# Pooled values times w_in: three float32r passes over split operands, or plain float32 products in the halves of a PSUM bank

## The chip, the cores and the metric

The kernel runs on one core of a Trainium2 chip. The metric is device time in microseconds (us); less is better. PE is TensorE, DVE is VectorE, ACT is ScalarE, POOL is GpSimd, and SP is the engine that issues the loads and stores here.

## The reference

```
a   = softmax(phi, axis=2)                       # over 576 positions, for each of 32 memory slots
k_m = einsum('bhsm,bhsd->bhmd', a, k)            # pooled keys,   32 x 64 per head
v_m = einsum('bhsm,bhsd->bhmd', a, v)            # pooled values, 32 x 64 per head
attn = softmax(q @ k_m.T / sqrt(64))             # 576 x 32 per head
x   = (attn @ v_m), heads side by side           # 2304 x 512
h   = x @ w_in; g = maximum(0.01 * h, h); y = g @ w_out          # d_ff 2048
out = ((y @ w_a) * (y @ w_b)) @ w_out2                           # d_ff 1536
```

There are 4 batches, 8 heads, and 2304 tokens (576 for each batch). Weights reach the kernel as 64-bit words, which it turns into float32 itself.

## The kernel before

**The tiling.** x is never formed. For each batch b and each chunk c of 512 columns of w_in (c = 0 to 3), the kernel multiplies the pooled values of the 8 heads by their rows of w_in. The result vw has 8 heads x 32 slots = 256 rows and 512 columns. Then h = attn @ vw (`h_unit`, L794) and y += g @ w_out (`y_unit`, L826) run over blocks of 288 tokens, two to a batch. The second MLP (`ab_unit`, `left_unit`, `o_unit`, `o_part`) follows.

**The split.** A product of full float32 accuracy is made of float32r operands: each is split into a high part (a copy that rounds to float32r) and a low part (the rest, by a subtraction), and PE makes three passes, high x high, high x low and low x high. So `weight` (L462) first joins the two words of each value into a float32 tile `cv` (loads by SP, two activations on ACT, then clamp, shift, join and add on DVE, some of them on POOL). Then it makes the split tile `win` of it (`hi` L501, `lo` L504). The pooled values are split into `vm_hi` and `vm_lo` (`ev_hi` L621, `ev_lo` L625), and vw itself into `vwh` and `vwl` when it leaves PSUM. The scores q @ k_m.T (`sc_part`, L661) and the pooling (`k_m`, L581) are plain float32 products without a split. `s_sc` writes two of them, of 64 rows each, into the two halves of one PSUM bank.

**The products in question.** A pair of heads has 64 rows of pooled values (32 slots for each head, the other head's half being zero). There are two ways before the change. For batches 0 and 1 in chunk 0, `vw_pair` (L723) fills a bank of 128 rows with two pairs: POOL copies the split values into tiles padded to 128 columns (`vp_hi`, `vp_lo`; `pad_hi`, `pad_lo`), and six passes of 256 columns add up in one bank. Everywhere else `vw_unit` (L749) takes two batches at a time, 64 rows each, in three passes of 256 (c = 0) or 512 columns. Each unit then leaves PSUM in four instructions of 64 rows, since two batches go to two tiles.

**The order.** All instructions are given to `Program.op` with planned costs, and `Program.order` fixes each engine's order ahead of the run. It goes by due time (`late`, less a slack from the table SLACK), by free tiles, and by the engine that would end sooner where two may do it. So a change of costs or of instructions can move other work. Each engine then runs its own list in order, and waits on semaphores.

**Names.** `ta`, `tz` are transposes of the softmaxed phi, `km` the pooled keys and values of four heads, `kvn` the same divided by the softmax sum, `kvt` its transpose; `kbd` holds the pooled keys for the scores `sc`; `sm`, `mx`, `sr`, `at`, `ahi`, `alo` are the stages of the attention softmax of a block and its split. In names such as `vw_0_1_0_1` the numbers are chunk, batch, column half and head group; in `h_0_2_0` chunk, block of 288 tokens, and quarter of the columns; `ta_1_0` and `sc_1_0_0` begin with the batch.

Of the kernel before, what the change touches and what calls it, by code (L numbers as in the profile page):

```python
# [10 lines left out]
F32 = mybir.dt.float32  # L11
# [13 lines left out]
FC = 512  # L25
# [307 lines left out]
def tile_mem_attention__leaky_mlp__bilinear_mlp(  # L333
# [61 lines left out]
    def two(n):  # L395

        return Port({"DVE": c_dve(n), "POOL": c_pool2(n)})

    def copy_by(n, psum=False):
        return (dict if psum else Port)({"ACT": c_act(n), "DVE": (c_dve(n) if psum else c_dve2(n)) + BIAS})  # L400

    def copy(e, dst, src):
        if e == "ACT":
            nc.scalar.copy(dst, src)  # L404
        else:
            nc.vector.tensor_copy(dst, src)
# [8 lines left out]
            small[key] = st_p.tile([P, cols], F32, name="_".join(map(str, key)))  # L415
        return small[key]

    tile_of(("vm_hi",), "slot", [4, B, 2 * M], F32R)
    tile_of(("vm_lo",), "slot", [4, B, 2 * M], F32R)
    VM = [("vm_hi",), ("vm_lo",)]  # L420


    VP = [("vp_hi",), ("vp_lo",)]
    for k in VP:
        tile_of(k, "slot", [4, 2, 4 * M], F32R)

# [6 lines left out]
    op(
        "POOL", 3.5, zeros,
        w=[("vm", b, g) for b in range(B) for g in range(2)] + [("vp", b, g) for b in range(2) for g in range(2)]
        + [("kbd", i, g) for i in range(2) for g in range(2)],
        tiles=VM + VP,
    )


# [21 lines left out]
    def weight(kind, c, k, after=()):  # L462
# [52 lines left out]
        op(Port({"DVE": 0.62, "POOL": 2.45}), 0, add, r=[("l", key)], w=[a], tiles=[cv], ahead=any_time)  # L515
        if kind in ("wa", "wb"):
            return
        if kind == "wout2" and by_seven(1, c):
            op(
# [5 lines left out]
        op(two(512), 0, lo, r=[a, ("hi", key)], w=[key], tiles=[cv, key], ahead=any_time, slack=SLACK[(kind + "0", k // 2) if first else kind])  # L525


    def kv_part(b, g):
# [84 lines left out]
        def wide(t, i):  # L613

            return [t[i * 64:i * 64 + 64, 2 * g + j, b, 2 * M * j + i * M:2 * M * j + i * M + M] for j in range(2)]

        def ev_k(T, e):
            for i in range(2):
                copy(e, own(kbd[b % 2], i), part(T, 0, i))

        def ev_hi(T, e):  # L621
            for i in range(2):
                copy(e, own(T[VM[0]], i, b), part(T, 1, i))

        def ev_lo(T):  # L625
            for i in range(2):
                nc.vector.tensor_tensor(
                    own(T[VM[1]], i, b), part(T, 1, i), own(T[VM[0]], i, b).bitcast(F32), op=ALU.subtract
                )

        def pad_hi(T):
            for i in range(2):
                for j, d in enumerate(wide(T[VP[0]], i)):
                    nc.gpsimd.tensor_copy(d, own(T[VM[0]], i, b)[:, j].bitcast(F32))

        def pad_lo(T):
            for i in range(2):
                for j, d in enumerate(wide(T[VP[1]], i)):
                    nc.gpsimd.tensor_copy(d, own(T[VM[1]], i, b)[:, j].bitcast(F32))

        op({"DVE": 0.5, "ACT": 0.45}, 0, ev_k, r=[o], w=[("kbd", b % 2, g)], tiles=[o])
        op({"ACT": 0.45, "DVE": 0.5}, 0, ev_hi, r=[o], w=[("vmh", b, g)], tiles=[o, VM[0]])
        op("DVE", 0.5, ev_lo, r=[o, ("vmh", b, g)], w=[("vm", b, g)], tiles=[o, *VM])
        if b < 2:
            op("POOL", 0.5, pad_hi, r=[("vmh", b, g)], w=[("vp", b, g)], tiles=[VM[0], VP[0]])
            op("POOL", 0.5, pad_lo, r=[("vm", b, g)], w=[("vp", b, g)], tiles=[VM[1], VP[1]])

    def q_load(b, g):
        if b > 0:
# [57 lines left out]
        )  # L707


    def vw(c, bs):  # L710

        n = FC if c else FC // 2
        m = len(bs) * 2 * M
        if len(bs) == 1:
            for x in range(2):
                for g in range(2):
                    vw_pair(bs[0], x, g)
            return
        for x in range(FC // n):
            for j in range(4):  # L720
                vw_unit(c, bs, x, j, n, m)

    def vw_pair(b, x, g):  # L723

        n = FC // 2
        o, w = ("vw", 0, b, x, g), ("win", 0, 2 * x + g)
        tile_of(o, "x", [n])
        cols = slice(x * n, (x + 1) * n)
        hk, lk = ("vwh", 0, b), ("vwl", 0, b)
        tile_of(hk, "slot", [2, FC], F32R)  # L730
        tile_of(lk, "slot", [2, FC], F32R)

        def prod(T):
            for j in range(2):
                for k, (v, i) in enumerate(((0, 0), (0, 1), (1, 0))):
                    nc.tensor.matmul(
                        T[o], T[VP[v]][:, 2 * g + j, b, :], T[w][:, i, j * n:(j + 1) * n],
                        start=(j == 0 and k == 0), stop=(j == 1 and k == 2),
                    )

        op("PE", 0.72, prod, r=[w, ("vp", b, g)], w=[o], tiles=[o, w, *VP], ahead=15.0)
        op(copy_by(n, True), 0, lambda T, e: copy(e, T[hk][:, g, cols], T[o]), r=[o], w=[(hk, g, x)], tiles=[o, hk])
        op(
            "DVE", c_dve(n),
            lambda T: nc.vector.tensor_tensor(T[lk][:, g, cols], T[o], T[hk][:, g, cols].bitcast(F32), op=ALU.subtract),
            r=[o, (hk, g, x)], w=[(lk, g, x)], tiles=[o, hk, lk], slack=SLACK["vw", 0, b],
        )

    def vw_unit(c, bs, x, j, n, m):  # L749
        o, w = ("vw", c, bs[0], x, j), ("win", c, j if c else 2 * x + j // 2)  # L750
        tile_of(o, "x", [n])
        cols, wcols = slice(x * n, (x + 1) * n), slice(0, FC) if c else slice(j % 2 * n, (j % 2 + 1) * n)
        to = slice((j % 2) * 64, (j % 2) * 64 + 64)

        def prod(T):
            for k, (v, i) in enumerate(((0, 0), (0, 1), (1, 0))):
                nc.tensor.matmul(  # L757
                    T[o][0:m], T[VM[v]][:, j, bs[0]:bs[0] + len(bs), :].rearrange("p b m -> p (b m)"), T[w][:, i, wcols],
                    start=(k == 0), stop=(k == 2),
                )  # L760

        op("PE", 0.01 + n * 1.27e-3, prod, r=[w] + [("vm", b, j // 2) for b in bs], w=[o], tiles=[o, w, *VM], ahead=15.0)
        for i, b in enumerate(bs):
            hk, lk = ("vwh", c, b), ("vwl", c, b)
            tile_of(hk, "slot", [2, FC], F32R)
            tile_of(lk, "slot", [2, FC], F32R)

            def hi(T, e, i=i, hk=hk):
                copy(e, T[hk][to, j // 2, cols], T[o][i * 64:(i + 1) * 64, :])

            def lo(T, i=i, hk=hk, lk=lk):
                nc.vector.tensor_tensor(  # L772
                    T[lk][to, j // 2, cols], T[o][i * 64:(i + 1) * 64, :], T[hk][to, j // 2, cols].bitcast(F32), op=ALU.subtract
                )

            op(copy_by(n, True), 0, hi, r=[o], w=[(hk, j, x)], tiles=[o, hk])
            op("DVE", c_dve(n), lo, r=[o, (hk, j, x)], w=[(lk, j, x)], tiles=[o, hk, lk], slack=SLACK["vw", min(c, 1), bs[0]])
# [16 lines left out]
    def h_unit(c, n, f, pos):  # L794
# [8 lines left out]
        def prod(T):  # L803
            for k in range(2):
# [490 lines left out]
    for c in range(NC1):  # L1295
        for k in range(4):
            weight("win", c, k)
        for bs in ([0], [1], [2, 3]) if c == 0 else ([0, 1], [2, 3]):
            vw(c, bs)
        for k in range(4):  # L1300
            weight("wout", c, k)
        for n in range(NBLK):
            for f in range(4):
                h_unit(c, n, f, (step, (-6, -5, -3, -1)[f]))
            for e in range(4):
                y_unit(c, n, e, (step + 1, (-4, -2, 0, 1)[e]))
            step += 1
# [80 lines left out]
```

## Time and profile before

| | |
|---|---|
| median of 3 runs | 807.0 us (806.95 to 807.73) |
| profiled execution | 804.98 us, of which the span from first to last instruction is 803.2 us |
| busy in the span | PE 778.4 us (97%), DVE 648.4 (81%), ACT 400.2 (50%), POOL 178.1 (22%) |
| granted TensorE clock | 0.998 of full speed, mean over the span |

"Busy" is the time in which an engine has an instruction in work. Matmuls overlap, so 97% for PE says that it rarely stood still, not that it ran at its peak. The windows and chains of the rows further down say more: they tell in which stretch an engine had gaps, and how long a piece of work took from its start to the start of the next.

### The profile page before, as it was taken

To read this page: it belongs to the slowest core of one execution; us is meant where nothing else is said; L and a number is where in the kernel's file an instruction comes from. 1 tells how busy PE (TensorE), PEld (TensorE's weight loads), DVE (VectorE), ACT (ScalarE), POOL (GpSimd) and SP (SyncE) were. 2 spreads that over 40 slices of the span, in tenths; PEclk is the share of its full clock that TensorE was granted. 3 is DMA by queue.
4 is the path that set the end of the run, shared out by engine and by line. 5 is a ranking of instruction groups with operands and counts; after the bars stand their busy time and mean duration, and the time that the engine had idled before them with its cause. 6 is when DMAs were issued, how large, how long until landed. Compare 5 with 4: busy or idle time off the path is not lost.

```text
span 803.2 us, 13329 instructions
## 1 busy us (share of the span) xinstructions
PE 778.4 (97%) x4898; PEld 695.9 (87%) x4898; DVE 648.4 (81%) x1240; ACT 400.2 (50%) x859; POOL 178.1 (22%) x274
## 2 busy tenths in 40 slices
PE   5789999999999999999999999999999989999998
PEld 4578899999999999999978888888888877888886
DVE  6998898889887988897756998998944665798955
ACT  5756786776657566644335544454411244232120
POOL 4632453033101420530100102341200111034200
PEclk9999999999999999999999999999999999999999
DMA  9995301174226232137887665665597778566402
GB/s 338 326 299 165 119 1 54 42 248 145 72 86 223 94 117 94 64 140 252 292 287 238 220 232 191 215 251 163 198 319 289 281 260 279 194 211 214 152 1 104
DMA packets 55216, 150.01 MB, mean 187 GB/s; under 512 B 6896, under 2 KB 20208, under 8 KB 55152
## 3 DMA queue, kind: packets, MB, share of 16 engines
q1 hardware_dynamic: 55152, 149.18, 53.9%
q8 instruction: 38, 0.62, 0.3%
q14 instruction: 26, 0.21, 0.1%
HBM read 103.55 MB, written 45.61 MB: 186 GB/s over the span
## 4 chain that ended last, share of the span: by engine, by line
PE 85%; DMA 6%; DVE 5%; issue 1%; ACT 1%; SPq 0%; ACTq 0%; DVEq 0%
PE y L836 24%; PE abx L1049 14%; PE o L1135 12%; PE h L806 12%; PE abz L1049 7%; PE os L1251 4%; PE aby L1049 3%; DMA k_yb_T<-yb_T 3%; PE vw L757 2%; PE b L1103 2%; PE a L1103 2%; DMA q<-in_qT_dram 1%; DMA k_wout<-wout 1%; PE sc L674 1%; PE km L586 1%
## 5 line engine op out<-in xcount | busy, mean ns | idle before, releaser
L836 PE MATMUL y<-g,wout 128*128 128x288 f32 x1536 | 219.5, 296 | 0.1
L836 PEld LDWEIGHTS y<-g,wout 128*128 128x128 f32 x1536 | 209.2, 188 | 3.3 <-issue 1.3
L1049 PE MATMUL abx<-yb_T,wo 128*128 128x512 f32 x432 | 110.2, 390 | 0.6 <-ACT t L1060 0.6
L1135 PE MATMUL o<-p,wout 128*128 128x512 f32 x384 | 94.8, 390 | 0.9 <-ACT oacc L404 0.9
L1049 PEld LDWEIGHTS abx<-yb_T,wo 128*128 128x128 f32 x432 | 80.0, 188 | 17.1 <-ACT t L1060 1.2
L1060 ACT COPY t<-abx 128x512 f32<-128x512 f32 x72 | 42.2, 586 | 97.4 <-PE abx L1049 97.4
L783 ACT ACTIVATE g<-h 128x288 fp32r<-128x288 f32 x128 | 52.6, 411 | 70.9 <-PE h L806 64.7
L1135 PEld LDWEIGHTS o<-p,wout 128*128 128x128 f32 x384 | 71.8, 188 | 16.6 <-ACT oacc L404 1.3
L806 PE MATMUL h<-ahi,vwh 128*128 128x288 f32 x256 | 76.9, 300 | 0.8 <-ACT ahi L404 0.8
L806 PE MATMUL h<-alo,vwh 128*128 128x288 f32 x256 | 76.3, 298 | 1.1 <-POOL alo L387 1.0
L806 PE MATMUL h<-ahi,vwl 128*128 128x288 f32 x256 | 76.0, 297 | 0.0
L848 DVE TENSOR_TENSOR acc<-y,acc 128x288 f32<-128x288 f32 x96 | 43.2, 454 | 19.6 <-PE y L836 18.6
L822 DVE TENSOR_TENSOR g<-t,g 128x288 fp32r<-128x288 f32 x100 | 48.5, 487 | 5.1 <-ACT t L783 4.7
L783 ACT ACTIVATE t<-h 128x288 f32<-128x288 f32 x128 | 52.1, 407 | 0.1
L806 PEld LDWEIGHTS h<-ahi,vwh 128*128 128x128 f32 x256 | 48.7, 190 | 3.1 <-issue 1.5
L806 PEld LDWEIGHTS h<-alo,vwh 128*128 128x128 f32 x256 | 48.7, 190 | 1.8 <-POOL alo L387 1.7
L1057 DVE TENSOR_TENSOR t<-abz,t 128x512 f32<-128x512 f32 x48 | 33.0, 688 | 20.6 <-ACT t L1060 10.3
L806 PEld LDWEIGHTS h<-ahi,vwl 128*128 128x128 f32 x256 | 48.6, 190 | 0.0
L772 DVE TENSOR_TENSOR vwl<-vw,vwh 64x512 fp32r<-64x512 f32 (+1 forms) x64 | 39.8, 621 | 7.6 <-ACT vwh L404 6.1
L404 ACT CAST vwh<-vw 64x512 fp32r<-64x512 f32 (+2 forms) x62 | 31.5, 509 | 21.3 <-PE vw L757 14.1
L1148 DVE TENSOR_TENSOR oacc<-o,oacc 128x512 f32<-128x512 f32 x40 | 27.5, 688 | 15.8 <-PE o L1135 15.3
L387 POOL TENSOR_TENSOR g<-t,g 128x288 fp32r<-128x288 f32 x28 | 25.0, 898 | 64.4 <-ACT t L783 55.6
(330 smaller groups left out, 1502.9 us busy)
## 6 DMA issues: line engine op xcount, KB each, us to landing
k_wo<-wo SPq DMA_DIRECT2D x32, 512.0 KB, 3.1
wo<-k_wo SPq DMA_DIRECT2D x32, 512.0 KB, 4.6
raw_wout<-in_w_out_dram SPq DMA_DIRECT2D x24, 512.0 KB, 4.9
raw_win<-in_w_in_dram SPq DMA_DIRECT2D x16, 512.0 KB, 5.5
kv<-in_kv_dram SPq DMA_DIRECT2D x16, 512.0 KB, 9.4
k_yb_T<-yb_T SPq DMA_DIRECT2D x8, 512.0 KB, 6.4
raw_wa<-in_w_a_dram SPq DMA_DIRECT2D x8, 512.0 KB, 4.6
raw_wb<-in_w_b_dram SPq DMA_DIRECT2D x8, 512.0 KB, 5.4
```

The source lines that it names most:

```text
L772: nc.vector.tensor_tensor(T[lk][to, j // 2, cols], T[o][i * 64:(i + 1) * 64, :], T[hk][to, j // 2, cols].bitcast(F32), op=ALU.subtract)
L783: nc.scalar.activation(dst, src, AF.Prelu, alpha=0.01)
L806: nc.tensor.matmul(T[o], T[w[u]][:, k, fs], T[a[v]][:, k, cols], start=(k == 0 and i == 0), stop=(k == 1 and i == 2))
L822: lambda T, e: engines[e].tensor_tensor(T[g][:, i, 1, :], T[t], T[g][:, i, 0, :].bitcast(F32), op=ALU.subtract),
L836: nc.tensor.matmul(T[o], w[:, u, es], g[:, v, :], start=(f == 0 and i == 0), stop=(f == 3 and i == 2))
L848: "DVE", c_dve(NB), lambda T: nc.vector.tensor_tensor(T[acc][:, e, :], T[o], T[acc][:, e, :], op=ALU.add),
L1049: nc.tensor.matmul(T[o], T[w][:, which, u, k * P:(k + 1) * P], T[ys[v]][:, k, :], start=first and k == 0 and x == 0, stop=k == 1 and x == ...
L1057: op("DVE", 0.69, lambda T: nc.vector.tensor_tensor(T[to], T[o], T[x], op=ALU.add), r=[o, x], w=[to], tiles=[o, x, to])
L1060: op("ACT", 0.59, lambda T: nc.scalar.copy(T[t], T[X]), r=[X], w=[t], tiles=[X, t])
L1103: nc.tensor.matmul(T[o], T[w][:, k // 2, u, k % 2 * P:(k % 2 + 1) * P], T[ys[v]][:, k, :], start=(k == 0 and x == 0), stop=(k == 3 and x = ...
L1135: nc.tensor.matmul(T[o], T[w][:, u, es], T[g][:, at, v, :], start=(x == 0 and k == 0), stop=(x == 1 and k == 2))
L1251: nc.tensor.matmul(T[o], lhs(T, u), T[g][:, v, :], start=k == 0, stop=k == 2)
```

## The change

All products of pooled values and w_in become plain float32 products of one batch: a unit holds two head pairs, one in each half of a PSUM bank, from one stationary tile of 64 columns each. The pooled values stay one float32 tile `vm`, and w_in stays in its float32 tile `cv`. The splits of both, the padded tiles, `vw_pair`, and the units of two batches go. vw is split as before when it leaves PSUM, now always 128 rows at a time. Two planned costs change as well: the zeroing (3.5 to 2.0) and `k_m` (1.5 to 0.95).

```diff
-    VM = [("vm_hi",), ("vm_lo",)]
-    VP = [("vp_hi",), ("vp_lo",)]
+    VM = ("vm",)
+    tile_of(VM, "slot", [4, B, 2 * M])
...
-        if kind not in ("wa", "wb"):
+        if kind not in ("wa", "wb", "win"):
             tile_of(key, "slot", [2, 512], F32R, heir_of=raw)
...
-        if kind in ("wa", "wb"):
+        if kind in ("wa", "wb", "win"):
             return
...
-        op("PE", 1.5, k_m, r=[(en, 0), (en, 1), *kvt, rest], w=[km], tiles=[en, *kvt, rest, km])
+        op("PE", 0.95, k_m, r=[(en, 0), (en, 1), *kvt, rest], w=[km], tiles=[en, *kvt, rest, km])
...
-        op({"ACT": 0.45, "DVE": 0.5}, 0, ev_hi, r=[o], w=[("vmh", b, g)], tiles=[o, VM[0]])
-        op("DVE", 0.5, ev_lo, r=[o, ("vmh", b, g)], w=[("vm", b, g)], tiles=[o, *VM])
-        if b < 2:
-            op("POOL", 0.5, pad_hi, r=[("vmh", b, g)], w=[("vp", b, g)], tiles=[VM[0], VP[0]])
-            op("POOL", 0.5, pad_lo, r=[("vm", b, g)], w=[("vp", b, g)], tiles=[VM[1], VP[1]])
+        op({"ACT": 0.45, "DVE": 0.5}, 0, ev_v, r=[o], w=[("vm", b, g)], tiles=[o, VM])
...
-    def vw(c, bs):
+    def vw(c, b):
         n = FC if c else FC // 2
...
+        for x in range(FC // n):
+            for g in range(2):
+                vw_unit(c, b, x, g, n)
+
+    def vw_unit(c, b, x, g, n):
+        o = ("vw", c, b, x, g)
         tile_of(o, "x", [n])
+        ws = [("cv", "win", c, 2 * g + j) for j in range(2)] if c else [("cv", "win", 0, 2 * x + g)]
...
         def prod(T):
             for j in range(2):
-                for k, (v, i) in enumerate(((0, 0), (0, 1), (1, 0))):
-                    nc.tensor.matmul(
-                        T[o], T[VP[v]][:, 2 * g + j, b, :], T[w][:, i, j * n:(j + 1) * n],
-                        start=(j == 0 and k == 0), stop=(j == 1 and k == 2),
-                    )
+                w = T[ws[j if c else 0]][:, 0, (0 if c else j * n):][:, :n].bitcast(F32)
+                nc.tensor.matmul(T[o][j * 64:(j + 1) * 64, :], T[VM][:, 2 * g + j, b, :], w, start=True, stop=True)
...
-        for bs in ([0], [1], [2, 3]) if c == 0 else ([0, 1], [2, 3]):
-            vw(c, bs)
+        for b in range(B):
+            vw(c, b)
```

The order of the instructions moves with it, at two places above all.

PE's list at the start, from the last pooling of batch 0 to the first products vw, before:

```order
L586 MATMUL km_0_1_237<-kvr_0_153,en_0_1_194 32x128 x4
L603 MATMUL kvt_0_0_262<-ident_69,kvn_0_0_258 128x128 x2
L603 MATMUL kvt_0_1_271<-ident_69,kvn_0_1_265 128x128 x2
L674 MATMUL sc_0_0_0_282<-q_0_0_0_230,kbd0_74 64x288 x2
L674 MATMUL sc_0_1_0_294<-q_0_1_0_235,kbd0_74 64x288 x2
L736 MATMUL vw_0_0_0_0_306<-win_0_0_144,vp_hi_111 128x256 x2
L736 MATMUL vw_0_0_0_0_306<-win_0_0_144,vp_lo_112 128x256
```

And the same place in the changed kernel:

```order
L595 MATMUL kvt_0_0_214<-ident_69,kvn_0_0_212 128x128 x2
L578 MATMUL km_0_1_225<-kv_0_1_0_179,en_0_1_181 32x128 x8
L578 MATMUL km_0_1_225<-kv_0_1_1_210,en_0_1_181 32x128 x8
L578 MATMUL km_0_1_225<-kvr_0_147,en_0_1_181 32x128 x4
L697 MATMUL vw_0_0_0_0_246<-cv_win_0_0_117,vm_109 64x256 x2
L697 MATMUL vw_0_0_1_0_253<-cv_win_0_2_132,vm_109 64x256 x2
L642 MATMUL sc_0_0_0_258<-q_0_0_0_217,kbd0_74 64x288 x2
L595 MATMUL kvt_0_1_266<-ident_69,kvn_0_1_251 128x128 x2
L697 MATMUL vw_0_0_0_1_277<-cv_win_0_1_124,vm_109 64x256 x2
L697 MATMUL vw_0_0_1_1_283<-cv_win_0_3_142,vm_109 64x256 x2
L642 MATMUL sc_0_1_0_287<-q_0_1_0_223,kbd0_74 64x288 x2
```

The first head group now goes through to its products and scores before the second one's transpose `kvt_0_1`, which stands behind two units vw and a score.

PE's list at the end of chunk 0, where the products of chunk 1 come in between the last units y, before (the fourth unit of the two batches follows two units y later):

```order
L836 MATMUL y_0_6_2_1924<-g_0_6_1_1784,wout_0_3_557 128x288 x3
L757 MATMUL vw_1_0_0_0_1943<-win_1_0_1834,vm_hi_109 128x512 x2
L757 MATMUL vw_1_0_0_0_1943<-win_1_0_1834,vm_lo_110 128x512
L757 MATMUL vw_1_0_0_1_1949<-win_1_1_1837,vm_hi_109 128x512 x2
L757 MATMUL vw_1_0_0_1_1949<-win_1_1_1837,vm_lo_110 128x512
L757 MATMUL vw_1_0_0_2_1961<-win_1_2_1856,vm_hi_109 128x512 x2
L757 MATMUL vw_1_0_0_2_1961<-win_1_2_1856,vm_lo_110 128x512
L836 MATMUL y_0_6_3_1966<-g_0_6_0_1708,wout_0_0_485 128x288 x3
```

And in the changed kernel, where the two units of one batch stand together, and two units y (eight rows, of which the first is shown) lie between them and the first h that needs them:

```order
L767 MATMUL y_0_6_2_1797<-g_0_6_1_1659,wout_0_3_495 128x288 x3
L697 MATMUL vw_1_0_0_0_1818<-cv_win_1_0_1073,vm_109 64x512
L697 MATMUL vw_1_0_0_0_1818<-cv_win_1_1_1102,vm_109 64x512
L697 MATMUL vw_1_0_0_1_1829<-cv_win_1_2_1312,vm_109 64x512
L697 MATMUL vw_1_0_0_1_1829<-cv_win_1_3_1367,vm_109 64x512
L767 MATMUL y_0_6_3_1836<-g_0_6_0_1604,wout_0_0_462 128x288 x3
...
L737 MATMUL h_1_0_0_1870<-ahi_0_352,vwh_1_0_1833 128x288
```

In chunks 1 to 3 there are twelve such places, one for each chunk and batch, each with two units. From the first unit of the second MLP on, PE's list is the same in both kernels.

## Rows read from the trace of the kernel before

**Rows 1.** The page's 40 equal slices: busy tenths, and the granted clock.

```profile
PE   5789999999999999999999999999999989999998
DVE  6998898889887988897756998998944665798955
PEclk9999999999999999999999999999999999999999
```

**Rows 2.** Windows: stretch, sum; busy PE, PEld, DVE, ACT, POOL; clock; DMA.

```profile
28.00:60.00 32.00, 25.81 (x230) 21.33 (x231) 31.42 (x77) 20.11 (x56) 16.14 (x32) 0.95 0.89 291
60.00:84.00 24.00, 24.00 (x296) 19.79 (x295) 20.12 (x63) 15.01 (x47) 4.30 (x5) 1.00 0.45 150
110.00:200.00 90.00, 90.00 (x663) 89.04 (x662) 79.98 (x158) 64.77 (x149) 32.21 (x47) 1.00 0.33 109
200.00:400.00 200.00, 199.95 (x1444) 196.12 (x1443) 171.05 (x330) 112.44 (x249) 41.31 (x61) 1.00 0.41 141
400.00:600.00 200.00, 198.75 (x1038) 170.81 (x1037) 163.51 (x290) 92.60 (x170) 33.85 (x44) 1.00 0.67 230
```

**Rows 3.** Chain that ended last, 108 to 345 us: start, us, what (c >= 1).

```profile
133.98 2.05 PE vw L757 x9
136.03 3.17 PE y L836 x24
139.20 0.68 PE vw L757 x3
```

**Rows 4.** The chain from 84 us on (c = 0).

```profile
84.29 1.07 PE vw L757 x9
```

**Rows 5.** The chain from 96 to 112 us, with the scores.

```profile
98.35 0.64 PE sc L674 x4
98.99 0.98 PE h L806 x6
99.97 1.59 PE y L836 x12
101.56 0.79 PE h L806 x6
...
105.55 1.60 PE h L806 x12
107.15 1.12 PE sc L674 x8
108.27 1.80 PE h L806 x12
```

**Rows 6.** The tile sc: duration in ns (least, median, most), first and last start.

```profile
L674 PE MATMUL sc<-q,kbd x64: 406/406/457, 19.5 to 107.9; 128*64 128x288 f32 x64
```

**Rows 7.** The chain from 60 to 67 us, the pooling of two head groups.

```profile
64.49 2.73 PE km L586 x80
```

**Rows 8.** DVE's groups between 5 and 60 us: busy us, mean ns | idle before.

```profile
L505 DVE TENSOR_TENSOR win<-cv_win,win 128x512 fp32r<-128x512 f32 x3 | 2.0, 679 | 0.0
L627 DVE TENSOR_TENSOR vm_lo<-kvt,vm_hi 64x64 fp32r<-64x64 f32 x8 | 1.7, 213 | 0.2
L406 DVE COPY kbd<-kvt 64x64 f32<-64x64 f32 x4 | 0.9, 222 | 0.8 <-ACT vm_hi L404 0.7
L406 DVE CAST win<-cv_win 128x512 fp32r<-128x512 f32 x1 | 0.4, 419 | 0.0
```

**Rows 9.** PE's timeline about 58 us: start, us; what ended the wait.

```profile
57.91 0.50 PE L736 MATMUL vw<-win,vp_hi 128*128 128x256 f32 x2 [1.40 <-DVE vwl L745]
...
59.44 0.60 PE L569 MATMUL ta<-ident,phi 128*128 128x128 f32 x4
59.80 0.38 PE L806 MATMUL h<-ahi,vwh 128*128 128x288 f32 x1
```

**Rows 10.** The tile vw: durations in ns as in rows 6.

```profile
L757 PE MATMUL vw<-win,vm_hi x64: 278/389/398, 84.1 to 336.8; 128*128 128x512 f32 x48, 128*128 128x256 f32 x16
L772 DVE TENSOR_TENSOR vwl<-vw,vwh x64: 378/684/696, 85.5 to 339.8; 64x512 fp32r<-64x512 f32 x48, 64x256 fp32r<-64x256 f32 x16
L404 ACT CAST vwh<-vw x62: 362/578/586, 22.7 to 338.5; 64x512 fp32r<-64x512 f32 x41, 64x256 fp32r<-64x256 f32 x13, 128x256 fp32r<-128x256 f32 x8
```

More of the change, by code (lines that the diff above doesn't have):

```diff
@@ L433, in tile_mem_attention__leaky_mlp__bilinear_mlp @@
     op(
[L434 to L437, printed above, removed]
+        "POOL", 2.0, zeros, w=[("vm", b, g) for b in range(B) for g in range(2)] + [("kbd", i, g) for i in range(2) for g in range(2)],
+        tiles=[VM],
     )
@@ L514, in weight @@
         op(Port({"DVE": 0.68}), 0, join, r=[raw], w=[a], tiles=[raw, cv], ahead=any_time)
-        op(Port({"DVE": 0.62, "POOL": 2.45}), 0, add, r=[("l", key)], w=[a], tiles=[cv], ahead=any_time)
-        if kind in ("wa", "wb"):
+        slack = SLACK[(kind + "0", k // 2) if first else kind]
+        op(Port({"DVE": 0.62, "POOL": 2.45}), 0, add, r=[("l", key)], w=[a], tiles=[cv], ahead=any_time, slack=slack if kind == "win" else 0.0)
+        if kind in ("wa", "wb", "win"):
             return
@@ L524, in weight @@
         op(copy_by(512), 0, hi, r=[a], w=[("hi", key)], tiles=[cv, key], ahead=any_time)
-        op(two(512), 0, lo, r=[a, ("hi", key)], w=[key], tiles=[cv, key], ahead=any_time, slack=SLACK[(kind + "0", k // 2) if first else kind])
+        op(two(512), 0, lo, r=[a, ("hi", key)], w=[key], tiles=[cv, key], ahead=any_time, slack=slack)
     def kv_part(b, g):
@@ L619, in ev_k, with ev_v @@
                 copy(e, own(kbd[b % 2], i), part(T, 0, i))
-        def ev_hi(T, e):
+        def ev_v(T, e):
             for i in range(2):
[L623 to L628, printed above, removed]
-                )
[L631 to L639, printed above, removed]
-        op({"DVE": 0.5, "ACT": 0.45}, 0, ev_k, r=[o], w=[("kbd", b % 2, g)], tiles=[o])
-        op({"ACT": 0.45, "DVE": 0.5}, 0, ev_hi, r=[o], w=[("vmh", b, g)], tiles=[o, VM[0]])
-        op("DVE", 0.5, ev_lo, r=[o, ("vmh", b, g)], w=[("vm", b, g)], tiles=[o, *VM])
-        if b < 2:
-            op("POOL", 0.5, pad_hi, r=[("vmh", b, g)], w=[("vp", b, g)], tiles=[VM[0], VP[0]])
-            op("POOL", 0.5, pad_lo, r=[("vm", b, g)], w=[("vp", b, g)], tiles=[VM[1], VP[1]])
+                copy(e, own(T[VM], i, b), part(T, 1, i))
+        op({"DVE": 0.5, "ACT": 0.45}, 0, ev_k, r=[o], w=[("kbd", b % 2, g)], tiles=[o])
+        op({"ACT": 0.45, "DVE": 0.5}, 0, ev_v, r=[o], w=[("vm", b, g)], tiles=[o, VM])
     def q_load(b, g):
@@ L707, in sc_part @@
         )
-    def vw(c, bs):
+    def vw(c, b):
         n = FC if c else FC // 2
[L713 to L718, printed above, removed]
-        for x in range(FC // n):
[L720 to L726, printed above, removed]
+        for x in range(FC // n):
+            for g in range(2):
+                vw_unit(c, b, x, g, n)
+    def vw_unit(c, b, x, g, n):
+        o = ("vw", c, b, x, g)
         tile_of(o, "x", [n])
+        ws = [("cv", "win", c, 2 * g + j) for j in range(2)] if c else [("cv", "win", 0, 2 * x + g)]
         cols = slice(x * n, (x + 1) * n)
-        hk, lk = ("vwh", 0, b), ("vwl", 0, b)
+        hk, lk = ("vwh", c, b), ("vwl", c, b)
         tile_of(hk, "slot", [2, FC], F32R)
@@ L734, in prod @@
             for j in range(2):
-                for k, (v, i) in enumerate(((0, 0), (0, 1), (1, 0))):
-                    nc.tensor.matmul(
-                        T[o], T[VP[v]][:, 2 * g + j, b, :], T[w][:, i, j * n:(j + 1) * n],
-                        start=(j == 0 and k == 0), stop=(j == 1 and k == 2),
-                    )
-        op("PE", 0.72, prod, r=[w, ("vp", b, g)], w=[o], tiles=[o, w, *VP], ahead=15.0)
+                w = T[ws[j if c else 0]][:, 0, (0 if c else j * n):][:, :n].bitcast(F32)
+                nc.tensor.matmul(T[o][j * 64:(j + 1) * 64, :], T[VM][:, 2 * g + j, b, :], w, start=True, stop=True)
+        op(
+            "PE", 0.03 + 4 * n / 2.4e3, prod, r=[("a", (k[1:])) for k in ws] + [("vm", b, g)], w=[o], tiles=[o, VM, *ws],
+            ahead=15.0,
+        )
         op(copy_by(n, True), 0, lambda T, e: copy(e, T[hk][:, g, cols], T[o]), r=[o], w=[(hk, g, x)], tiles=[o, hk])
@@ L745, in vw_pair @@
             lambda T: nc.vector.tensor_tensor(T[lk][:, g, cols], T[o], T[hk][:, g, cols].bitcast(F32), op=ALU.subtract),
-            r=[o, (hk, g, x)], w=[(lk, g, x)], tiles=[o, hk, lk], slack=SLACK["vw", 0, b],
+            r=[o, (hk, g, x)], w=[(lk, g, x)], tiles=[o, hk, lk], slack=SLACK["vw", min(c, 1), b - b % 2 if c else min(b, 2)],
         )
[L749 to L777, printed above, removed]
     PASSES = ((0, 0), (0, 1), (1, 0))
@@ L812, in h_unit @@
             r=[(n_, b, k, x) for n_ in ("ahi", "alo") for k in range(2)] + [
-                (u, j, 0 if c else f // 2) for u in w for j in range(4 if c or b > 1 else 2)
+                (u, j, 0 if c else f // 2) for u in w for j in range(2)
             ],
```

9 lines of the change are left out of this document (1 added, 8 removed).

## Prediction

> **What bounds the kernel now.** I read the page's slices first. PE shows nines from the fourth slice on, at a granted clock of nine tenths or more, and only the first three slices (60 us) are thinner; DVE stays below nine in most slices [rows 1]. So there are two regimes, and the windows show where they meet. Between 28 and 60 us DVE is busy 31.42 of 32 us and PE 25.81: here the end is set by DVE's list. From 60 us PE is busy 24.00 of 24, from 110 us 90.00 of 90, from 200 us 199.95 of 200 [rows 2]. In that second regime an engine other than PE can give nothing back, and each microsecond that PE's list gains or loses moves the end. PE's timeline shows the seam: the last wait of note ends at 57.91 us, put down to DVE's `vwl`, and at 59.80 us the first h of block 2 (`h_0_2_0`) starts [rows 9]. That h is my marker: what the change does before it counts only by how much earlier or later the marker comes, and what it does behind it counts in PE time.
>
> **PE behind the marker, chunks 1 to 3: the main term.** Before, a pair of batches costs 12 passes of 512 columns. The chain has nine of them in 2.05 us and three in 0.68 us, with units y on either side at their usual length [rows 3]; six such groups are 6 x 2.73 = 16.4 us. After, there are 12 bursts (chunk and batch) of two units; a unit is two plain float32 products of 64 rows, in the two halves of a bank. The trace has that form at 288 columns, the scores `sc`: 64 records for 32 products, so two passes for each and four records for a pair [rows 6]. Four records take 0.64 us in the chain, eight take 1.12, so a pair in a row costs 0.48 us. That is 1.67 ns a column, and the records of 406 ns lie over one another: the halves do run together, else eight could not end in 1.12 us. Each change of form costs besides: 0.64 - 0.48 = 0.16 us ahead, and the work behind it is longer, six passes of h 0.98 us where the usual is 0.79, twelve 1.80 where the usual is 1.60 [rows 5]. So a burst has 0.16 + 0.19 = 0.35 us on top, whatever its length (the same 0.16 and 0.20 come out of the burst of eight). At 512 columns a pair is 0.48 x 512 / 288 = 0.853 us, a burst 2 x 0.853 + 0.35 = 2.06 us, twelve are 24.7 us: **+8.3 us**.
>
> The cost at 512 columns is not in the trace, so it needs bounds. From below: a pass need not grow in proportion. The pooling has 80 records of 128 columns in 2.73 us, four 32-column strips together, so 20 passes of 0.137 us [rows 7]; a line through (128, 0.137) and (288, 0.24) gives 0.38 us at 512, a pair 0.77, twelve bursts 22.7 us, +6.3. From above: the second unit of a burst may pay the change of form again, 12 x 0.35 = 4.2 us more, +12.5. I take the proportional value, since 288 columns is the nearer row and the extra 0.35 did not repeat within the burst of eight.
>
> **A rule against the rows.** The rows give 0.24 us for a pass of 288 plain float32 columns [rows 5], and 2.05 / 9 = 0.228 us for a float32r pass of 512 [rows 3]: a plain column costs about twice a float32r one, and a product needs two passes. The Trainium skill, "TensorE: Matmul & The Clock Gate", Part 2 (What happens when you issue a matmul), has throughput as purely N cycles, one moving column a cycle, and names no exception for plain float32. The trace disagrees for the scores; if the products went by that rule, the sum would be the one of the third rival below.
>
> **PE behind the marker, chunk 0, batches 2 and 3.** Before, 24 passes of 256 columns at 1.07 / 9 = 0.119 us: 2.85 us [rows 4]. After, eight units at 0.48 x 256 / 288 = 0.427: 3.41 us. By the order, bursts of plain float32 behind the marker go from eight (scores alone) to nine, since some units stand next to a score: +0.35. Together **+0.9 us**.
>
> **Ahead of the marker.** Batches 0 and 1 of chunk 0 take eight units of 6 x 0.119 = 0.71 us before, and 0.43 after. PE has 6 us of gaps between 28 and 60 us [rows 2], so this I cost at nothing; without that cover it would give about 1 us, with the changes of form. What counts is DVE's list up to the marker. It loses three low parts of w_in (2.0 us), one high part (0.4) and eight low parts of the pooled values (1.7): 4.1 us [rows 8]. A few scalings and sums change places between DVE and POOL, which I put at zero, within 1 us. POOL's copies into the padded tiles go too, but DVE's `vwl` was the last to be waited for, not they [rows 9].
>
> Against that stands the new order. `kvt_0_1` now waits behind two units and a score: 2 x 0.43 + 0.64 = 1.5 us. Queued behind it on PE are the other two units, the second score, and everything after; on DVE the second `kbd`, which already had DVE's only noted wait of 0.7 us [rows 8], and the softmax of the second head group. I charge the whole 1.5 us. Also, the four transposes `ta` that ran at 59.44 to 59.80 us, ahead of the marker [rows 9], stand behind it now: 0.4 us. The marker comes 4.1 - 1.5 - 0.4 = **2.2 us earlier**, in effect. Bounds: nothing, if DVE waits for all that it saved, to 5 us, if it never waits and the moves help. On SP, the two loads of q for the second block of batch 0 now go ahead of four loads of k and v of batch 1; those four come later by the 0.6 MB of the two (128 x 576 float32 each), about 2 us at 291 GB/s [rows 2], and PE wants them only after the four h of block 0. I cost that at nothing.
>
> **What I cost at nothing.** In chunks 1 to 3 the 48 low parts of 64 rows (684 ns each) become 24 of 128 rows, and the copies on ACT halve as well [rows 10]; twelve more tiles of w_in lose their split. That is over 20 us of DVE and ACT work, all of it where PE stood still 0.05 of 200 us [rows 2]. The second MLP's list on PE does not change.
>
> **The sum.** +8.3 + 0.9 - 2.2 = +7.0 us. The profiled execution took 804.98 us, 1.8 more than its span of 803.2, and becomes 812.0. It lies 2.0 below the median of the runs, 807.0, so the median becomes **814.0 us**. A measurement of this kernel can tell about 0.2% (1.6 us) from no change.
>
> **Rivals.**
> *Late evictions (slower still).* `h_1_0_0` needs both units of its batch, split. Two units y lie between, 3.17 us [rows 3]. The last unit then needs an ACT copy of 578 ns and a DVE subtraction of 684 ns [rows 10], 1.3 us, which leaves 1.9 us for hand-overs and for what stands ahead on DVE, busy 171 of 200 us [rows 2]. For it speaks that busy share; against it, that before four units had to be evicted in halves and PE did not wait. If each of the twelve came 0.5 us late, 6 us more: 820.
> *No early gain (slower).* The wait for `kvt_0_1` spreads, and DVE idles for all that it saved: +8.3 + 0.9 + 0.4 = +9.6, 816.6. DVE being full between 28 and 60 us speaks against it [rows 2].
> *Plain float32 at one column a cycle (faster).* If a pass of 512 cost the 0.228 us of a float32r one, a burst would be 4 x 0.228 + 0.35 = 1.26 us, twelve 15.1, -1.3; the eight units of 256 would take 8 x 0.24 + 0.35 = 2.3, -0.6. With the early gain -4.1: 803. It decides from a pass under about 0.30 us, where the sum is zero. The scores speak against it, 0.24 us at only 288 columns [rows 5].
> *A large early gain (no change or faster).* The place is DVE's list up to the marker. It must bring the marker forward by 9.2 us to undo the rest, and more to be faster; then 807 or less. For it: DVE was the bound there nearly without a gap. Against it: its list loses 4.1 us, and PE's gaps between 28 and 60 us come to 6.2 us in all [rows 2].
>
> **How the numbers follow.** The forecast (slower by 2 to 13 us) 0.68, late evictions 0.10, no early gain 0.07, one column a cycle 0.04, a large early gain 0.11 (no change 0.07, faster 0.04). So slower 0.85, same 0.07, faster 0.08. The bounds of the terms give 6.3 + 0.9 - 5.0 = +2.2 at the low end, 809; at the high end 12.5 + 0.9 with no early gain is +13.4, 820. From 809 to 820 holds the forecast, the missing early gain and half of the late evictions, 0.8 in all.
>
> **What would show it.** In the changed kernel's profile: two units of vw in a row at about 1.9 us in the chain with the units y behind them 0.2 us longer; a plain float32 pass of 512 columns with starts 0.43 us apart; `h_0_2_0` starting near 57 us; PE busy without gaps from there; DVE's busy time down by over 20 us. I am wrong if a pass of 512 columns takes near 0.23 us, if the marker comes near 50 us or not earlier at all, or if PE waits ahead of the first h of each chunk for `vwl`.

## The result, and the profile after

The changed kernel takes **811.87 us** (median of 4 runs, 810.26 to 813.02), the kernel before beside it 807.37: ratio 1.0054, 95% interval 1.0032 to 1.0076. Timed once more later (`after2`, 12 runs) it took 811.12 beside 807.13, ratio 1.0043, 1.0024 to 1.0062. By these ratios it is slower by 3.5 to 4.4 us; the forecast was 7.0 us slower, 814.0. The profiled execution took 810.26 us with a span of 808.5.

The page's slices, as in [rows 1]:

```profile
PE   5699999999999999999999999999999999999998
DVE  5998787898887884677766889999954666798955
PEclk8799999999999999999999999999999999999999
```

The same windows as in [rows 2]:

```profile
28.00:60.00 32.00, 27.55 (x234) 20.93 (x234) 30.05 (x78) 21.34 (x60) 14.27 (x18) 0.85 0.89 301
60.00:84.00 24.00, 24.00 (x232) 19.01 (x232) 18.89 (x53) 15.79 (x47) 5.73 (x7) 1.00 0.30 102
110.00:200.00 90.00, 90.00 (x652) 83.81 (x652) 77.06 (x157) 59.07 (x138) 25.55 (x32) 1.00 0.44 153
200.00:400.00 200.00, 200.00 (x1437) 186.70 (x1436) 150.01 (x302) 93.35 (x215) 22.41 (x34) 1.00 0.34 113
```

From 60 to 400 us PE has no gap, and DVE has 21 us less to do between 200 and 400 us than before: 150.01 against 171.05 [rows 2]. Over the whole span DVE is busy 620.2 us instead of 648.4, and the end came later all the same. It goes with PE's list.

The chain of waits, at the first burst of chunk 1 and at one later on:

```profile
132.25 1.57 PE y L767 x12
133.82 1.87 PE vw L697 x8
135.69 3.36 PE y L767 x24
...
164.10 1.58 PE y L767 x12
165.68 0.79 PE h L737 x6
166.47 1.87 PE vw L697 x8
168.34 1.78 PE y L767 x12
```

This is the piece to read. The eight records of a burst (two units of two halves, two passes each) take 1.87 us, and twelve passes of y take 1.78 behind it where elsewhere they take 1.57 or 1.58. A burst costs 1.87 + 0.20 = 2.07 us; the prediction had 2.06. A pair of batches thus costs 2 x 2.07 = 4.14 us on PE, where it cost 2.05 + 0.68 = 2.73 [rows 3].

The tile vw, as in [rows 10]: half as many evictions, 128 rows each at the same duration.

```profile
L697 PE MATMUL vw<-cv_win,vm x160: 379/592/644, 19.7 to 357.7; 128*64 128x512 f32 x96, 128*64 128x256 f32 x64
L706 DVE TENSOR_TENSOR vwl<-vw,vwh x40: 383/682/693, 20.8 to 359.3; 128x512 fp32r<-128x512 f32 x24, 128x256 fp32r<-128x256 f32 x16
```

PE's timeline where `h_0_2_0`, the marker, starts (the last row), and the rows ahead of the first h of all:

```profile
32.87 1.23 PE L642 MATMUL sc<-q,kbd 128*64 128x288 f32 x4 [3.30 <-ACT en L404]
34.03 0.61 PE L737 MATMUL h<-ahi,vwh 128*128 128x288 f32 x1
...
57.84 0.30 PE L737 MATMUL h<-ahi,vwl 128*128 128x288 f32 x1
57.98 0.29 PE L737 MATMUL h<-ahi,vwh 128*128 128x288 f32 x1
```

The marker stands at 57.98 us, 1.8 earlier than in [rows 9], though PE waited 3.30 us for a score (the profile puts the wait down to the copy `en` on ACT) and the granted clock was 0.85 between 28 and 60 us where it had been 0.95.

Three times tell where the microseconds went, in every run below: the start of the marker, the start of the second MLP's first product (`abx`), and the end of the span. Between the marker and `abx` lies only PE's list of the first MLP.

| | marker | abx | marker to abx | abx to end | span |
|---|---|---|---|---|---|
| before | 59.80 | 386.74 | 326.94 | 416.46 | 803.2 |
| before2 | 61.60 | 388.65 | 327.05 | 414.57 | 803.2 |
| changed | 57.98 | 393.26 | 335.28 | 415.23 | 808.5 |
| after2 | 58.05 | 393.34 | 335.29 | 415.77 | 809.1 |

For one and the same kernel the list between the two repeats to 0.1 us from one execution to the next: it grew by 8.3 us. Between kernels it is less exact: `late_split_en`, below, has the same records behind the marker as `late_split` and takes 328.96 us where `late_split` takes 327.81 and 327.72. The marker and the second MLP do not repeat so well (1.8 and 1.9 us between two executions of the same kernel), so what they give has to be judged by the timed runs.

### The profile page after: what moved, and what is told of

Same layout as the page of the kernel before. It is cut to its first block, busy times and chain, and to the rows that moved or that the text cites. A ratio compares the mean times of both kernels' runs of the same rounds, so it can differ in the third digit from the quotient of the medians.

```text
span 808.5 us, 13110 instructions
## 1 busy us (share of the span) xinstructions
PE 786.3 (97%) x4914; PEld 683.3 (85%) x4914; DVE 620.2 (77%) x1196; ACT 374.7 (46%) x810; POOL 135.9 (17%) x187
## 2 busy tenths in 40 slices
DMA packets 55215, 150.01 MB, mean 186 GB/s; under 512 B 6896, under 2 KB 20208, under 8 KB 55152
## 4 chain that ended last, share of the span: by engine, by line
PE 92%; DMA 4%; DVE 2%; issue 1%; SPq 1%; ACT 0%; ACTq 0%
PE y L767 25%; PE abx L980 16%; PE o L1066 12%; PE h L737 12%; PE abz L980 8%; PE os L1182 4%; PE vw L697 4%; PE aby L980 4%; PE a L1034 2%; PE b L1034 2%; PE km L578 1%; DMA phi<-in_phiT_dram 1%; DMA k_yb_T<-yb_T 1%; DMA kv<-in_kv_dram 1%; PE sc L642 1%
## 5 line engine op out<-in xcount | busy, mean ns | idle before, releaser
L753 DVE TENSOR_TENSOR g<-t,g 128x288 fp32r<-128x288 f32 x108 | 51.9, 482 | 17.0 <-ACT t L714 16.4
L404 ACT CAST p<-t 128x512 fp32r<-128x512 f32 x31 | 19.3, 621 | 39.3 <-DVE t L1012 32.8
L980 PE MATMUL abx<-yb_B,wo 128*128 128x512 f32 x144 | 36.9, 392 | 0.0
L980 PE MATMUL abz<-yb_B,wo 128*128 128x512 f32 x144 | 36.8, 391 | 0.0
```

Source lines behind the costliest of these rows:

```text
L753: lambda T, e: engines[e].tensor_tensor(T[g][:, i, 1, :], T[t], T[g][:, i, 0, :].bitcast(F32), op=ALU.subtract),
L980: nc.tensor.matmul(T[o], T[w][:, which, u, k * P:(k + 1) * P], T[ys[v]][:, k, :], start=first and k == 0 and x == 0, stop=k == 1 and x == ...
```

## The experiments

Ratios are to the kernel before, run beside each, with 95% intervals.

| run | median us | before us | ratio | interval |
|---|---|---|---|---|
| late_split | 803.05 | 806.25 | 0.9961 | 0.9939 to 0.9983 |
| early_split | 813.69 | 806.25 | 1.0080 | 1.0055 to 1.0106 |
| plain128 | 806.95 | 806.25 | 1.0004 | 0.9989 to 1.0020 |
| twice | 829.76 | 806.25 | 1.0280 | 1.0258 to 1.0302 |
| km15 | 814.60 | 806.72 | 1.0094 | 1.0065 to 1.0122 |
| before_km | 806.06 | 806.72 | 0.9986 | 0.9971 to 1.0001 |
| late_split_en | 804.51 | 806.72 | 0.9978 | 0.9963 to 0.9993 |
| mixed | 804.75 | 806.72 | 0.9973 | 0.9955 to 0.9990 |
| after2 | 811.12 | 807.13 | 1.0043 | 1.0024 to 1.0062 |
| late_split2 | 802.78 | 807.13 | 0.9948 | 0.9928 to 0.9968 |
| idle_split | 804.78 | 807.13 | 0.9974 | 0.9960 to 0.9987 |
| before2 | 805.00 (one) | 806.77 (one) | | |

### The two halves of the change, one at a time

`late_split` keeps the change in chunk 0 and undoes it in chunks 1 to 3.

```diff
-        if kind in ("wa", "wb", "win"):
+        if kind in ("wa", "wb") or (kind, c) == ("win", 0):
             return
...
+        op(copy_by(512), 0, vs_hi, r=rs, w=[("vsh", b)], tiles=[VM, VS[0]], ahead=25.0)
+        op("DVE", c_dve(512), vs_lo, r=[*rs, ("vsh", b)], w=[("vs", b)], tiles=[VM, *VS], ahead=25.0)
...
+            for k, (v, i) in enumerate(((0, 0), (0, 1), (1, 0))):
+                nc.tensor.matmul(
+                    T[o], T[VS[v]][:, j, bs[0]:bs[0] + 2, :].rearrange("p b m -> p (b m)"), T[ws[0]][:, i, :],
+                    start=(k == 0), stop=(k == 2),
+                )
```

> Chunk 0 is left as in the changed kernel; in chunks 1 to 3 the products go back to three float32r passes over a pair of batches, w_in split, the pooled values split once in SBUF. Theory (the loss sits in the products of chunks 1 to 3, on PE's list): the traces of the two kernels have 6.7 us of it there, so 811.9 - 6.7 = 805.2 us, between 803.6 and 806.5, about 2 us under the kernel before, since the earlier marker is kept. Rival (the loss comes from the new start of the program, a lower granted clock and a wait of 3.3 us there): 811 to 812 us.

`early_split` does the opposite: chunk 0 as before, the plain products in chunks 1 to 3.

```diff
+            nc.vector.tensor_tensor(
+                T[VF][:, :, b:b + 2, :], T[VM[0]][:, :, b:b + 2, :].bitcast(F32), T[VM[1]][:, :, b:b + 2, :].bitcast(F32), op=ALU.add
+            )
...
+                w = T[ws[j]][:, 0, :].bitcast(F32)
+                nc.tensor.matmul(T[o][j * 64:(j + 1) * 64, :], T[VF][:, 2 * g + j, b, :], w, start=True, stop=True)
```

> Chunk 0 as in the kernel before (split, padded tiles); in chunks 1 to 3 the plain float32 products of the changed kernel, from pooled values put together again by one addition per two batches. Theory (the products of chunks 1 to 3): 807.4 + 6.7 = 814.1 us, between 813 and 815.7, and the marker h_0_2_0 back near 59.8 us. Rival (the start): 807 to 808 us.

Both came out as the theory has it, and the rival fell. The four corners fit together: putting in the late half alone makes the kernel slower by 0.8% (6.5 us), taking it out of the changed kernel makes it faster by 1.0054 - 0.9961 = 0.9% (7.5 us). The early half alone gives 0.39% (3.1 us), and 0.52% when it was timed again (`late_split2`, below). The marker of `early_split` came at 63.43 us, not at the 59.8 that was expected of the same instructions, which is why `before2` was run. From marker to `abx` it takes 334.63 us, 7.7 more than before; `late_split` 327.81, 7.5 less than the changed kernel.

### What a burst is made of

`plain128` has both batches of a pair as the 128 columns of one plain float32 product, so that no 64-column form is left in chunks 1 to 3. The result leaves PSUM in halves of 64 rows again.

```diff
+            nc.tensor.matmul(
+                T[o], T[VM][:, j, bs[0]:bs[0] + 2, :].rearrange("p b m -> p (b m)"), T[ws[0]][:, 0, :].bitcast(F32),
+                start=True, stop=True,
+            )
```

> As the changed kernel, but in chunks 1 to 3 one plain float32 product has both batches of a pair as its 128 columns, so the form of 64 columns in two halves is used in chunk 0 and the scores alone; the results are evicted in halves of 64 rows, as before. The number of passes in a row stays 24 pairs at 0.853 us. If the 0.35 us of a burst (0.1 ahead, 0.2 in the work behind) belongs to the change between 64 and 128 columns: 12 x 0.35 = 4.2 us less, 807.7 us, and the y behind the products back to 1.57 us for twelve. If it belongs to the change between float32 and float32r: six bursts instead of twelve, 2.1 us less, 809.8 us, y still longer. If it belongs to neither: 811.9 us.

The chain of `plain128` at the same place:

```profile
133.16 1.57 PE y L796 x12
134.73 2.58 PE vw L718 x6
137.31 4.80 PE y L796 x36
142.11 0.86 PE vw L718 x2
142.97 3.16 PE y L796 x24
```

and that of `late_split`, with three float32r passes instead of two plain ones:

```profile
133.41 1.57 PE y L800 x12
134.98 2.06 PE vw L722 x9
137.04 4.80 PE y L800 x36
141.84 0.70 PE vw L722 x3
142.54 3.15 PE y L800 x24
```

Six plain passes take 2.58 us and two take 0.86, 0.43 each; the y behind them are as long as behind float32r passes (4.80 and 4.80, 3.16 and 3.15). So plain float32 beside float32r costs no changeover, and the 0.36 us of a burst belongs to the change between 64 and 128 stationary columns: 0.16 ahead, which is 1.87 less the 1.71 that eight records take in `twice` below, and 0.20 behind. Without it the time falls from 1.0054 to 1.0004, by 4.0 us (by 3.1 from the 1.0043 of `after2`), nearest to the first case of the expectation (12 x 0.35 = 4.2). The list shows only a part of this: from marker to `abx` `plain128` takes 333.00 us, 2.3 less than the changed kernel. The products, with three passes on either side, take 3.7 us less, and the other passes 1.4 us more; 0.9 of that lies in four long passes of y at 223.5 and 387.7 us, where PE stopped for DVE. The Trainium skill, "TensorEngine Tiling (Array Packing)", Key Properties, says that changing the tiling mode drains the engine, without a price. No run here shows the drain itself; a price of 0.36 us there and back agrees with it.

`twice` issues every product of chunks 1 to 3 of the changed kernel two times.

```diff
-            for j in range(2):
+            for j in [0, 1] * (2 if c else 1):
```

> As the changed kernel, but each product of chunks 1 to 3 is issued twice, the second over the first. Theory (PE's list sets the end, a pair in a row costs 0.853 us): 24 x 0.853 = 20.5 us more, 832.4 us. Rival (part of the pair's time lies in waits that a longer list fills): less than 15 us more.

Its chain at the first burst:

```profile
131.34 1.57 PE y L767 x12
132.91 3.58 PE vw L697 x16
```

Eight records more take 3.58 - 1.87 = 1.71 us, which is two pairs at 0.855 us: the rival of a wait that a longer list would fill fell here. From marker to `abx` the kernel takes 356.08 us, 20.8 more than the changed one (expected 20.5); the time rose by 18 to 19 us (1.0280 against 1.0054 and 1.0043), 2 us less than the list. In its trace the marker came 0.9 us earlier and the second MLP was 0.7 shorter, both within what these show between two executions of one kernel.

### The start

`km15` puts the planner's figure for the pooling back in the changed kernel (`op("PE", 0.95, k_m` to `1.5`), and `before_km` makes that edit alone in the kernel before.

> The changed kernel with the planner's figure for the pooling put back from 0.95 to 1.5. By its order the last two scores of block 0 then stand behind the first four h, so the 3.3 us that PE waited for one of them at 29 to 33 us cannot stand ahead of those h. Theory (the loss is the products of chunks 1 to 3, the figure only moves work that DVE's list covers): 811 to 812.5 us. Rival (the new figure and its order at the start cost the 3.3 us): 808 to 809 us.

> The kernel before with nothing but the planner's figure for the pooling changed from 1.5 to 0.95. Theory: 806 to 807.5 us, no difference from the kernel before. Rival (the figure is a part of what moved the marker): 2 us or more to either side.

`before_km` showed no difference, as expected. `km15` was slower than expected, 814.6 us. Its trace says that the rival was wrong in kind: the order did put the first h earlier, and the marker came later.

```profile
28.86 0.61 PE L737 MATMUL h<-ahi,vwh 128*128 128x288 f32 x1 [1.34 <-ACT ahi L404]
...
59.27 0.38 PE L737 MATMUL h<-ahi,vwh 128*128 128x288 f32 x1
```

The first h starts at 28.86 us instead of 34.03, the marker at 59.27 instead of 57.98. PE's wait of 3.30 us at 29 us was covered. That its loss is 0.4 to 0.5% above the changed kernel's (intervals 1.0065 to 1.0122 and, for `after2`, 1.0024 to 1.0062) is not explained by the 1.3 us of the marker alone; it stays open.

`late_split_en` asks the same question of the other kernel: `slack=4.0 if b == 1 else 0.0` on the copies of `tz`.

> late_split with 4 us of slack on the copies of the transposed tails (tz to en) of batch 1, so that ACT does them earlier and no score waits for their bank; by the order the second transposes of the pooled values also go ahead of the first score. Theory (DVE's list sets the marker, PE's wait at 30 us is covered): the first h starts 2 to 4 us earlier, the marker within 1 us, 802 to 803.5 us. Rival (the wait lies on the path): 799 to 801 us.

The first h starts at 29.50 us (35.23 in `late_split`, 32.96 in `late_split2`), the marker at 57.88 (59.13 and 56.89), and the time is not better: 804.51 us, 0.9978, above the ranges of both theory and rival. That an earlier first h brings nothing held; the forecast of the time did not. The score now waits 2.9 us for the same copies, elsewhere.

`mixed` takes batches 2 and 3 of chunk 0 back to float32r passes as well (`for b in range(2): vw(c, b)`, and `vw_pairs` for the pair).

> late_split with plain float32 for batches 0 and 1 of chunk 0 alone; batches 2 and 3 of chunk 0 also go back to float32r passes over the pair, as in the kernel before. Theory (the early gain is DVE's shorter list, and plain products cost on PE's full list): the term of chunk 0 comes back, 0.9 us, 802.1 us. Rival (splitting w_in of chunk 0 puts 1.5 to 4 us back on DVE's list ahead of the marker): 803.5 to 806 us.

No gain: 0.9973. From marker to `abx` it takes 327.88 us against 327.81. PE now waits 0.84 us for a bank, but that is not the whole account: from the marker up to the first h of chunk 1 `mixed` takes 85.50 us and `late_split` 86.40, so 0.9 us did come back in spite of the wait. It is lost again behind, where the two lists have the same records and `mixed` takes 242.38 us against 241.41; why stays open.

```profile
88.84 1.08 PE L801 MATMUL y<-g,wout 128*128 128x288 f32 x7
90.76 0.47 PE L723 MATMUL vw<-win,vm_hi 128*128 128x256 f32 x2 [0.84 <-DVE vwl L738]
```

The time lies where the rival put it, but the marker, at 58.68 us, lies between those of `late_split` and `late_split2`, so it was not shown to be the rival's doing; and 0.9973 (0.9955 to 0.9990) cannot be told from `late_split`'s 0.9961.

### Whether the start's gain is DVE's

> The changed kernel once more, on the chip and beside the runs on which the next two are timed, since it was timed four times so far and its marker and that of other kernels with the same start differ by up to 2 us from one execution to another. If the effects add up (products of chunks 1 to 3 +6.5 to +7.5 us, start -2 to -3): 4 to 5 us over the kernel before, ratio 1.005 to 1.006. If km15's 1.0094 shows the spread rather than its edit: 1.007 or more.

> late_split once more, beside the others: if the gain of the start is real, 2 to 3.5 us under the kernel before, 6.5 to 7.5 us under the changed kernel.

Both repeated, each a little faster than expected: the changed kernel 1.0043, `late_split` 0.9948. `late_split` is the version that beats both kernels, the kernel before by 3.1 and 4.2 us in the two comparisons.

`idle_split` puts the split of chunk 0 back without using it.

```diff
-        op(two(512), 0, lo, r=[a, ("hi", key)], w=[key], tiles=[cv, key], ahead=any_time, slack=slack)
+        op(two(512), 0, lo, r=[a, ("hi", key)], w=[key, a] if (kind, c) == ("win", 0) else [key], tiles=[cv, key], ahead=any_time, slack=slack)
...
+                nc.vector.tensor_tensor(own(T[VD], i, b), part(T, 1, i), own(T[VM], i, b), op=ALU.subtract)
```

> late_split with the split work of chunk 0 put back (high and low parts of its w_in, low parts of the pooled values) though the plain products do not use it; the products wait for it as before, and by the order the head of the program is the kernel before's again. Theory (the gain of the start is the 4.1 us of DVE's list that went): the gain goes, h_0_2_0 back to 60 us or later, 806 to 808 us. Rival (the gain comes from PE's shorter products or the smaller tiles): 803 to 804 us.

It came out between the two cases: 804.78 us, 0.9974. DVE's groups between 5 and 60 us show that the work is there again, 4.2 us in these two rows:

```profile
L501 DVE TENSOR_TENSOR win<-cv_win,win 128x512 fp32r<-128x512 f32 x4 | 2.5, 683 | 0.0
L621 DVE TENSOR_TENSOR vm_idle<-kvt,vm 64x64 f32<-64x64 f32 x8 | 1.7, 212 | 0.1
```

Of the early gain of 0.39 and 0.52%, 0.13 and 0.26 are lost again with these 4.2 us (0.9974 against 0.9961 and 0.9948; the intervals overlap), so half or more of it stays with the work put back. The trace does not put the loss on DVE's list ahead of the marker: the marker stands at 58.97 us, between the 59.13 and 56.89 of `late_split`, and from there to `abx` it takes 329.11 us, 1.3 more than `late_split`, in an order that has moved as well. So it is not shown that the length of DVE's list is a part of the gain, and what makes the gain has to be looked for elsewhere.

A candidate stands in [rows 9]: the last unit of batch 1 waits for a PSUM bank until DVE has done a low part. It does so in `before2` (first fence) and, with the same instructions, in `early_split` (second fence) as well; the last row of each is the marker.

```profile
59.72 0.50 PE L736 MATMUL vw<-win,vp_hi 128*128 128x256 f32 x2 [1.41 <-DVE vwl L745]
...
61.60 0.38 PE L806 MATMUL h<-ahi,vwh 128*128 128x288 f32 x1
```

```profile
61.53 0.50 PE L738 MATMUL vw<-win,vp_hi 128*128 128x256 f32 x2 [1.39 <-DVE vwl L747]
...
63.43 0.38 PE L832 MATMUL h<-ahi,vwh 128*128 128x288 f32 x1
```

`idle_split` and the kernels with plain products at the start have no such wait ahead of the marker. But `before_km` has none either, by its order, and its marker stands at 61.80 us all the same. So this wait is not the gain by itself.

> The kernel before once more, for its marker: it stood at 59.80 us in the one trace so far, and at 63.43 us in early_split, whose program is the same up to there. If the start gains 3 us or more, h_0_2_0 stands at 60.5 us or later; if 59.80 is usual, near 59.8, and the gain is the 1.8 us of the first comparison. Behind the marker the time to the first product of the second MLP should be the 326.9 us of before within 0.5 us.

`before2` has its marker at 61.60 us, so 59.80 was an early execution, and 327.05 us from marker to `abx`, as expected.

These two traces have the same records in the same order on PE, so they also tell where the 1.8 us between their markers come from. The window from 45 to 47 us lies within the same three units y in both, `before` in the first line and `before2` in the second (columns as in [rows 2]):

```profile
45.00:47.00 2.00, 2.00 (x18) 2.00 (x17) 1.90 (x8) 0.40 (x1) 0.89 (x6) 1.00 1.03 324
45.00:47.00 2.00, 2.00 (x10) 2.00 (x10) 1.86 (x9) 0.00 (x0) 1.09 (x6) 0.50 1.00 297
```

The granted clock is at its upper level (2.4 GHz) in the one and at its lower (1.2 GHz) in the other, and PE has 10 passes in work instead of 18. Shortly before PE had stood still for `kvt` in both, 2.33 and 1.43 us. Record by record, `before2` is 0.23 us late at the scores behind that wait and 1.80 us late three microseconds further on, and it keeps these 1.80 us up to the marker. In `early_split`, whose list is the same up to the marker, the same units y add 1.55 us to a delay of 2.05. The wait for DVE's low part just ahead of the marker is as long in all three, 1.40, 1.41 and 1.39 us. So DVE comes later by what PE lost, and the marker follows PE's clock too, not DVE's list alone. Between 40 and 50 us the granted clock is 1.00 in both traces of the changed kernel and of `late_split`, in `plain128`, `twice`, `mixed` and `before`, and 0.66 to 0.83 in `before2`, `before_km`, `early_split`, `km15`, `late_split_en` and `idle_split`. It is a candidate for the early gain, and for what `idle_split` lost of it; no run changes the clock by itself, so this stays open.

## Why the prediction came out as it did

**Direction and mechanism: right.** The loss is PE's list in chunks 1 to 3, the gain is the start, and they add up: late half +6.5 to +7.7 us, early half -2.1 to -4.2. Each comes from differences of the ratios above: the late half from `early_split` alone and from the changed kernel less `late_split`, the early half from `late_split` alone and from the changed kernel less `early_split`.

**The burst: right in each part.** 2.07 us measured, 2.06 forecast; the pass of 512 columns 0.43 us, as the proportion from the scores had it, so the line through the 128-column passes (0.38), the bound from below, was too low. The changeover came once a burst, so the upper bound fell too.

**Chunks 1 to 3: right at the products, too large by 0.6 to 0.8 us in all.** Forecast +8.3, measured +7.5 (changed kernel less `late_split`) and +7.7 (`early_split` less before) between marker and `abx`. Counted from start to start, the products with three passes on either side cost 8.2 and 8.3 us more in these two pairs, as the sum has it; the other passes of h and y take 0.7 us less in both, and the sum has no term for them. Of that, 0.4 us are three long passes of y between the old groups of chunks 2 and 3 (at 221.7, 303.7 and 304.0 us in `late_split`), which the new lists do not have; the rest stays open. The y behind the old groups are not longer as such. Around the lines of [rows 3], whose 24 passes take 3.17 us, the chain of before has:

```profile
132.39 1.59 PE y L836 x12
...
139.88 4.76 PE y L836 x36
```

**Chunk 0 behind the marker: +1.3 forecast (0.9, and 0.4 for the transposes), +0.9 measured** (327.81 in `late_split` against 326.94), but by a sum of two. From the marker up to the first h of chunk 1, where the lists differ by eight records of vw and four transposes, `late_split` takes 86.40 us and before 84.68, 1.7 more. Behind it, with the same records, `late_split` takes 0.9 less (241.41 against 242.27); `late_split_en` has 242.37 there, so this is not the chunk's doing, and its cause stays open.

**The marker: the gain was put too small, by how much stays uncertain.** The sum has it 2.6 us earlier before the 0.4 that moves behind it. One pair of traces gives 1.8, the means of two each 60.70 - 58.02 = 2.7, and the timed runs 2.1 to 4.2 for the early half less its +0.9 on the list, that is 3.0 to 5.1. Over all traces whose chunk 0 is in full the changed kernel's (57.98, 58.05, 59.13, 56.89, 58.88 in `plain128` and 57.06 in `twice`) the mean is 58.0, and over the three with the start of before 61.6, so 3.6. The charge of 1.5 us for `kvt_0_1` was not seen as such: `late_split_en`, where `kvt_0_1` goes ahead of the first score again, has no earlier marker. That DVE's list alone makes the early gain was not borne out: `idle_split` puts the work back and keeps half of the gain or more. And PE's passes ahead of the marker, which the prediction cost at nothing, do count there: 1.57 us by the granted clock in one place of `before2`. So as far as the size of this term came out near, that is luck in part: its reason is not shown.

Together: the list behind the marker was forecast at 8.3 + 0.9 + 0.4 = +9.6 us and measured at +8.3, which is 1.3 of the 2.6 to 3.5 us by which 7.0 lies above the measured 4.4 and 3.5. The rest lies with the marker, if the 3.6 of the traces or the 3.0 to 5.1 of the timed runs hold.

**Costed at nothing: held.** 28 us less of DVE and 25 less of ACT (400.2 to 374.7) bought nothing behind the marker.

**The rivals.** Late evictions fell: PE is busy 200.00 of 200 us, with no wait ahead of a chunk's first h. No early gain fell by `late_split`, and one column a cycle by the pass of 0.43 us. For that one, the Trainium skill, "FP8 and Floating Point Precision", TensorE Precision Notes, gives true float32 four passes through the array; the trace shows two records to a product, 0.86 us for both at 512 columns, which at a granted clock of 1.00 (2.4 GHz) is four cycles a column, so the price agrees with that section. A large early gain fell: the marker would have had to come 9.2 us earlier.

The signs announced were there: two units at 1.87 us, y 0.20 longer behind them, passes 0.43 apart, DVE down by 28 us. The marker at 57.98 and 58.05 is a microsecond later than the 57 announced, since the first execution of before, from which it was counted, was early.

## What to carry to other kernels

Where one engine is full, count an operand's split against passes of that engine alone: a plain float32 product replaced three float32r passes of 0.23 us by two of 0.43, and all the DVE work that it saved was hidden. The same edit paid at the start, where PE has gaps and DVE is nearly full, though why it paid there is not settled; so decide stage by stage, which is what `late_split` does. And before a small early term is trusted, trace the unchanged kernel more than once: its start alone moved by 1.8 us.

## What the hardware showed that was not expected

- Plain float32 runs at 0.43 us for 512 columns with 128 stationary columns too, and two halves of 64 run together in that time. The halves gain nothing over the full width, and cost 0.36 us per burst where the work around them has 128 columns.
- The start does not repeat: with the same instructions up to it, the marker stood at 59.80, 61.60 and 63.43 us, while in before the 327 us behind it repeat to 0.1 us. Of the first 1.8 us, 1.57 arise in one stretch of scores and y at a granted clock of 0.50 instead of 1.00.
- An execution of one and the same kernel (before) took between 804.5 and 810.9 us, which is why gains under 0.2% could not be told apart even with 12 runs.
